# Four of six mask row blocks through a table in DRAM, and the later weights' low parts off TensorE: sparse attention with a two-layer MLP on one core

## The chip, the cores and the metric

The kernel runs on one core of a Trainium2 chip. PE is TensorE (matmuls), DVE is VectorE, ACT is ScalarE, POOL is GpSimd, and SP is SyncE, whose queue issues all the large DMAs here. The metric is the device time of one execution in microseconds, as a median of several runs.

## The reference

Block-sparse attention over 4 batches and 8 heads, 768 tokens, head size 64; its output, as 3072 tokens of 512, goes through a two-layer MLP with a leaky rectifier.

```python
scores = scale * np.matmul(q, k.transpose(0, 1, 3, 2))
mask = np.abs(blk_i - blk_j) <= window          # blocks of 32 tokens, 24 of them
mask = mask | (blk_i == 0) | (blk_j == 0) | (blk_i == n_blocks - 1) | (blk_j == n_blocks - 1)
for qb in range(n_blocks):
    for kb in sampled_blocks[qb]:
        mask[qb * block:(qb + 1) * block, kb * block:(kb + 1) * block] = True
scores = np.where(mask, scores, -1000000000.0)
attn = softmax(scores)
x = (attn @ v), as [3072, 512]
h = x @ w_in                                     # w_in 512 x 2048
g = np.maximum(h, 0.0) + alpha * np.minimum(h, 0.0)
out = g @ w_out                                  # w_out 2048 x 512
```

All inputs and the output are float32.

## The kernel before

**Split numbers.** Every float32 operand of a large product is scaled by a power of two and split into two float16 parts, a high part (the rounded value) and a low part (what is left), and a product is three matmuls: high with high, and each low with the other's high. So each operand needs two instructions: `times` (L431) writes the high part, `rest` (L439) the low part. On DVE the low part is one instruction (L441, reading source and high part), on POOL it is two (L443 scales in place, L444 subtracts).

**The weights.** w_in and w_out come as 16 tiles each, `f` = 0 to 15 (the profile's tensors wi and wo; a tile's raw data stands in a part of wo or in a buffer raw). `raw_to_f32` (L1055) turns a raw tile into float32 in three steps: n1 on DVE (L930), n2 on ACT (L935) or DVE (L940), n3 on DVE (L946). Two or four tiles give a norm over matmuls (gram, L956), and from it the scale. Then `prep_wi` (L1079) and `prep_wo` (L1101) make the two parts. The high part is on ACT, DVE or POOL (L433, L435, L437). The low part of all 16 tiles of w_in, and of the first eight of w_out, comes over PE: POOL scales an identity by the tile's scale (`emit_sid`, L1022), a float32 matmul of it with the tile (L1033) and a float16 matmul of a negative identity with the high part (L1034) leave the difference in PSUM, and ACT copies it out (L1038). The last eight of w_out take `emit_w_lo` on DVE (L441).

**The mask.** A table of 24 x 24 blocks is made on POOL and DVE. PE widens its columns to 768 keys (L380), ACT copies that to `tcol` (L393), 24 rows. For each of the six row blocks t of `bias` (128 queries each, interleaved: query 6p + t), two matmuls with a selection matrix repeat the rows (`mask_rows_pe`, L385) and ACT writes 0 or a large negative number (L401). The code for fewer row blocks on PE stands there already (`MROWS < NT`, L403): a table `rows` of 768 x 768 in DRAM, written from `tcol` with each row 32 times (`mask_store`) and read back by query (`mask_load`). With MROWS = 6 it is not run.

**Attention.** The work is cut in 12 chunks of two query tiles, three to a batch; a chunk has four units (pairs of heads), a unit four steps (one head and one query tile). For each two steps PE makes the scores (L653, L659), DVE adds `bias` and takes the maximum (L669), ACT exponentiates (L676), DVE inverts the sum (L687), p is split into two parts (L433 or L437, then L441 or L443 and L444), SP transposes p by DMA (L704), and at the end of a unit PE multiplies with v (L730); ACT and DVE split that into x (L741, L746).

**The MLP.** For a chunk, eight steps j: PE multiplies x with two tiles of w_in (`emit_up`, L1149, 24 matmuls), DVE applies the rectifier (L1159, L1160), ACT and POOL split the result (L1165, L1170), PE multiplies with two tiles of w_out (`emit_down`, L1191). At the first of them everything of the weights' scales must be there (`emit_gsc`, L993 to L983), since they are one factor of the rectifier.

**What sets the order.** All of this is given to `Plan` as operations with a priority, a choice of engines with costs in us (a pair of numbers marks a step that shares a port between DVE and POOL), dependencies and buffers. `Plan.run` (L119) goes through a time of its own, gives each ready operation to the engine that would end it soonest by these costs (weighted by PREF, and PREF0 up to 130 us), and the kernel's instructions are issued in that order. Each engine then runs its list in order. The constants at L28 to L64 are the priorities and costs.

## Time and profile before

| | |
|---|---|
| median of 3 runs | 816.78 us (816.24 to 818.37) |
| profiled execution, its own time | 818.19 us |
| its span | 816.5 us |
| mean granted clock of PE | 0.985 |
| PE busy | 781.6 us (96%) |
| DVE, ACT, POOL busy | 604.9 (74%), 576.0 (71%), 429.9 us (53%) |
| DMA | 135.35 MB moved, mean 166 GB/s |

Times are from the span's start, in microseconds; instructions that a row groups carry their mean in ns. Short instructions overlap a little on their engine, so a sum of durations is larger than the busy time. A float32 matmul appears as two rows (x2 for one).

### The profile page before, as it was taken

The page shows a single profiled execution, that of the slowest core. Times are in us where ns is not written, and L with a number is a line of the kernel's source. Part 1 is how long each engine was busy: PE and PEld are TensorE (multiplying, and loading weights), DVE is VectorE, ACT ScalarE, POOL GpSimd, SP SyncE. Part 2 cuts the span into 40 slices and gives each one's busy share as a digit, 9 for nine tenths or more (in the row PEclk, how much of TensorE's full clock was granted, in tenths as well). Part 3 has the DMA queues.
Part 4 walks back from the last instruction along what each step waited for, and adds up shares of the span by engine and source line. Part 5 has one row for each costly group of instructions (what it writes and reads, how often), then busy time and mean ns, then how long its engine had stood idle before and what let it go on. Part 6 is the DMA issues. An engine that isn't in the chain of part 4 may idle for free.

```text
span 816.5 us, 16929 instructions
## 1 busy us (share of the span) xinstructions
PE 781.6 (96%) x6335; PEld 504.1 (62%) x6335; DVE 604.9 (74%) x1279; ACT 576.0 (71%) x1041; POOL 429.9 (53%) x360
## 2 busy tenths in 40 slices
PE   6848899999999999999999999999999999999997
PEld 4423365766766666666666666666666666676764
DVE  6898998887689777797687787958687888734231
ACT  6888997897577778876677878736587888724111
POOL 6475786575336555644355655544265656624121
PEclk9978999999999999999999999999999999999999
DMA  9997996987985979879787979629686887643000
GB/s 331 325 310 208 191 184 146 205 161 162 220 193 122 169 162 194 183 153 199 160 174 142 183 179 209 136 77 193 154 204 157 171 171 151 115 97 84 28 1 26
DMA packets 384722, 135.35 MB, mean 166 GB/s; under 512 B 349028, under 2 KB 377728, under 8 KB 384640
## 3 DMA queue, kind: packets, MB, share of 16 engines
q1 hardware_dynamic: 384576, 134.26, 74.8%
q8 instruction: 49, 0.80, 0.4%
q14 instruction: 33, 0.27, 0.1%
q0 software_dynamic: 64, 0.02, 0.0%
HBM read 35.67 MB, written 6.29 MB: 51 GB/s over the span
## 4 chain that ended last, share of the span: by engine, by line
PE 87%; DVE 4%; ACT 3%; POOL 2%; issue 1%; DMA 1%; POOLq 0%; ACTq 0%; DVEq 0%
PE h L1149 30%; PE o L1191 29%; PE sp L730 12%; PE sp L653 7%; PE sp L659 5%; PE d L1033 3%; ACT wo L935 1%; DVE e L669 1%; DMA kf<-in_k_dram 1%; PE d L1034 1%; POOL ph L444 1%; DVE n L930 1%; PE gram L956 0%; DVE ph L441 0%; POOL e L443 0%
## 5 line engine op out<-in xcount | busy, mean ns | idle before, releaser
L1149 PE MATMUL h<-x,wi 128*128 128x256 f16 x2304 | 267.2, 273 | 0.0
L1149 PEld LDWEIGHTS <-wi 128*128 128x128 f16 x2304 | 222.1, 98 | 46.9 <-issue 10.1
L1170 POOL TENSOR_TENSOR gl<-g,gh 128x512 f16<-128x512 f32 x96 | 115.7, 1205 | 220.3 <-ACT gh L1165 192.2
L1191 PE MATMUL o<-wo,gh 128*128 128x512 f16 x768 | 228.9, 380 | 0.0
L669 DVE CUSTOM_DVE_ANT_0 e<-sp,bias,cs 128x768 f32<-128x768 f32 x192 | 191.2, 1010 | 34.7 <-PE sp L659 16.6
L676 ACT ACTIVATE e<-e,nm 128x768 f32<-128x768 f32 x192 | 177.4, 925 | 18.6 <-DVE nm L669 18.4
L444 POOL TENSOR_TENSOR ph<-e,ph 128x768 f16<-128x768 f32 x96 | 171.6, 1788 | 8.0
L433 ACT ACTIVATE ph<-e,rs 128x768 f16<-128x768 f32 x181 | 164.4, 926 | 10.2 <-DVE rs L687 4.9
L443 POOL TENSOR_SCALAR e<-e,rs 128x768 f32<-128x768 f32 x96 | 92.4, 962 | 112.4 <-ACT ph L433 104.9
L1165 ACT CAST gh<-g 128x512 f16<-128x512 f32 x96 | 59.1, 616 | 125.6 <-DVE g L1160 106.0
L1191 PE MATMUL o<-wo,gl 128*128 128x512 f16 x384 | 145.5, 379 | 0.3 <-POOL gl L1170 0.3
L1159 DVE SCALAR_TENSOR_TENSOR g<-h,am 128x512 f32<-128x512 f32 x96 | 66.1, 689 | 78.3 <-PE h L1149 72.2
L1191 PEld LDWEIGHTS <-gh 128*128 128x128 f16 x768 | 70.5, 98 | 82.2 <-issue 6.3
L441 DVE SCALAR_TENSOR_TENSOR ph<-e,rs,ph 128x768 f16<-128x768 f32 x96 | 111.8, 1164 | 8.9 <-ACT ph L433 8.8
L730 PE MATMUL sp<-pt,v 128*64 128x256 f16 x1728 | 103.5, 274 | 0.0
L730 PEld LDWEIGHTS <-v 128*64 128x64 f16 x1728 | 90.6, 110 | 15.7 <-issue 15.0
L1160 DVE SCALAR_TENSOR_TENSOR g<-h,gsc,g 128x512 f32<-128x512 f32 x96 | 72.1, 751 | 3.4
L1191 PEld LDWEIGHTS <-gl 128*128 128x128 f16 x384 | 37.5, 98 | 46.0 <-POOL gl L1170 0.8
L653 PEld LDWEIGHTS <-qt 128*128 128x128 f16 x384 | 37.6, 98 | 29.3 <-issue 7.5
L653 PE MATMUL sp<-kt,qt 128*128 128x512 f16 x192 | 47.5, 330 | 3.6 <-DVE nm L669 3.6
L741 ACT ACTIVATE x<-sp 128x256 f16<-128x256 f32 x48 | 18.3, 380 | 43.6 <-DVE nm L669 25.1
L659 PE MATMUL sp<-kt,qt 64*128 64x512 f16 x192 | 48.2, 332 | 0.0
(152 smaller groups left out, 725.7 us busy)
## 6 DMA issues: line engine op xcount, KB each, us to landing
wo<-in_moe_w_in_dram SPq DMA_DIRECT2D x16, 512.0 KB, 6.4
raw<-in_moe_w_out_dram SPq DMA_DIRECT2D x16, 512.0 KB, 6.6
kf<-in_k_dram SPq DMA_DIRECT2D x16, 384.0 KB, 3.9
qf<-in_q_dram SPq DMA_DIRECT2D x12, 512.0 KB, 4.8
vf<-in_v_dram SPq DMA_DIRECT2D x16, 384.0 KB, 5.3
out_dram<-ob SPq DMA_DIRECT2D x24, 256.0 KB, 2.3
ks<-kt SPq DMA_DIRECT2D x28, 192.0 KB, 3.3
pt<-ph SPq DMA_TRANSPOSE x192, 3.5
```

Of the source, the lines that this page charges most:

```text
L433: nc.scalar.activation(dst, src, AF.Copy, scale=scale)
L441: nc.vector.scalar_tensor_tensor(dst, src, scale, hi, ALU.mult, ALU.subtract)
L443: nc.gpsimd.tensor_scalar(tmp, src, scale, 1.0, ALU.mult, ALU.mult)
L444: nc.gpsimd.tensor_tensor(dst, tmp, hi, ALU.subtract)
L653: nc.tensor.matmul(T["sp", n + i][:, a:z], T["qt", u][:, h, i, :], (ks, kt)[i][:, h, a:z], start=True, stop=False)
L659: nc.tensor.matmul(T["sp", n + i][:, a:z], T["qt", u][r, h, i, :], (kt, ks)[i][r, h, a:z], start=False, stop=True)
L669: nc.vector.tensor_tensor_reduce(T["e", n], T["sp", n], bias[:, t0 + j % w, :], scale=T["cs", c][:, hp : hp + 1], scalar=3.0e38, op0=ALU.a ...
L676: nc.scalar.activation(T["e", n], T["e", n], AF.Exp, bias=T["nm", n], scale=-1.0, accum_out=T["su", n])
L730: nc.tensor.matmul(av[h * D : (h + 1) * D, : n * P], v2[:, h, t, vv, :], T["pt", u, h][:, pl * NT + t, :], start=(m == 0), stop=(m == len( ...
L1149: nc.tensor.matmul(ph[:, i, :], win(w, f, ct), x[:, ct, :], start=(m == 0), stop=(m == len(terms) - 1))
L1170: nc.gpsimd.tensor_tensor(T["gl", c, j], T["g", c, j], T["gh", c, j], ALU.subtract)
L1191: nc.tensor.matmul(T["o", c][t], g[:, i, t * P : (t + 1) * P], wout(w, f), start=(i == 0 and m == 0 and j in first_j), stop=(i == 1 and m ...
```

## The change

The mask: MROWS goes from 6 to 2, so that row blocks 0 and 1 come from PE and ACT as before, and blocks 2 to 5 from the table in DRAM: POOL scales `tcol`, SP writes it with each row 32 times (768 x 768 in bfloat16), and SP reads four row blocks back into `bias`.

The weights: tiles 8 to 15 of w_in take their low parts from `emit_w_lo` on DVE or POOL; the last eight of w_out may now take it on POOL too.

The planner: an operation may have a `lead` (the time after which its DMA is taken to start); the costs are other, and nearly all constants of priority and preference. In the first 22 steps the low part of p may go to DVE or POOL by the planner's choice for each step (`PL0` "d"), where steps had alternated between that choice and DVE alone. A buffer `pa`, not used with HALF = 0, is dropped from the pools.

```diff
-V_WA = -4.856569
-W_WA = 1.529176
+V_WA = 2.696075
+W_WA = 0.554437
...
-PL0 = "dv"
+PL0 = "d"
...
-SLOW = 1.12
+SLOW = 1.02
...
+WI_PE = 8
...
-MROWS = 6
-M_PR = 0.0
+MROWS = 2
+M_PR = 8.0
...
-                        events.append((now + c + 1.0, o.n, "dma", o))
+                        events.append((now + (c + 1.0 if o.lead is None else o.lead), o.n, "dma", o))
...
-    MAX4 = {"DVE": (0.55, 0), "ACT": 0.88, "POOL": 0.95}
-    LOW4 = {"DVE": (0.94, 0), "POOL": (1.1, 1.7)}
+    MAX4 = {"DVE": (0.55, 0), "ACT": 0.88, "POOL": 0.92}
+    LOW4 = {"DVE": (0.96, 0), "POOL": (0.94, 1.52)}
+    LOWW = {"DVE": (0.67, 0), "POOL": (0.75, 1.24)}
...
-            o_sid = plan.op(p + OFF["wh"], {"POOL": 0.5}, lambda g=g: emit_sid(g), [gs[-1]], [sb])
+            if 2 * g < WI_PE:
+                o_sid = plan.op(p + OFF["wh"], {"POOL": 0.41}, lambda g=g: emit_sid(g), [gs[-1]], [sb])
             for y in (2 * g, 2 * g + 1):
...
+                if y >= WI_PE:
+                    prev = o_wi[y] = plan.op(p + OFF["wc"], LOWW, lambda e, y=y: emit_w_lo(e, "wi", y), [o])
+                    continue
                 db = plan.buf("o")
...
-            o_wo[y] = plan.op(p - 3 + 0.1 * (y % HF) + OFF["oh"], {"DVE": (0.67, 0)}, lambda e, y=y: emit_w_lo(e, "wo", y), [o])
+            o_wo[y] = plan.op(p - 3 + 0.1 * (y % HF) + OFF["oh"], LOWW, lambda e, y=y: emit_w_lo(e, "wo", y), [o])
```

Since the planner's costs and constants change, the order moves everywhere; three places matter to the prediction. Line numbers of the changed kernel are up to six higher than those of the kernel before.

PE, at the first up matmul of the MLP, before: the last matmul with v of the fourth unit, a low part of w_in (a scaled identity with a tile, then the negative identity with the high part), and the first up matmul.

```order
L730 MATMUL sp_74<-pt,v_710 64x256
L1033 MATMUL d<-wi,sid 128x512
L1034 LDWEIGHTS wi
L1034 MATMUL d<-wi 128x512
L1149 LDWEIGHTS wi
L1149 MATMUL h<-x,wi 128x256
```

The same place after:

```order
L732 MATMUL sp_74<-pt,v_676 64x256
L1035 MATMUL d<-wo,sid 128x512
L1036 LDWEIGHTS wi
L1036 MATMUL d<-wo,wi 128x512
L1155 LDWEIGHTS wi
L1155 MATMUL h<-x,wi 128x256
```

The first up matmul stands at the same place in both, behind 11 pairs of scores and four units of v; ahead of it stand 14 low parts of w_in before and 8 after, and behind it two before and none after. The low part next to it is now one of w_out.

SP, about the fifth to the tenth load of weights, before (kt, vf, ks, qf are tiles of k, v, swapped k and q; wo takes raw tiles of w_in):

```order
L561 DMA_TRANSPOSE kt<-kn 128x12x128
L469 DMA wo<-in_moe_w_in_dram 128x4x256 x3
L469 DMA vf<-in_v_dram 128x2x384
L561 DMA_TRANSPOSE kt<-kn 128x12x128
L469 DMA vf<-in_v_dram 128x2x384
L469 DMA raw<-in_moe_w_out_dram 128x1024
L469 DMA ks<-kt 64x1536 x2
L469 DMA wo<-in_moe_w_in_dram 128x4x256
L469 DMA raw<-in_moe_w_out_dram 128x1024 x3
L469 DMA qf<-in_q_dram 128x8x128
```

And after:

```order
L563 DMA_TRANSPOSE kt<-kn 128x12x128
L471 DMA wo<-in_moe_w_in_dram 128x4x256
L471 DMA vf<-in_v_dram 128x2x384
L409 DMA rows<-tcol 768x1x768
L471 DMA wo<-in_moe_w_in_dram 128x4x256
L563 DMA_TRANSPOSE kt<-kn 128x12x128
L471 DMA vf<-in_v_dram 128x2x384
L471 DMA wo<-in_moe_w_in_dram 128x4x256
L471 DMA raw<-in_moe_w_out_dram 128x1024
L471 DMA ks<-kt 64x1536 x2
L471 DMA raw<-in_moe_w_out_dram 128x1024 x2
L471 DMA qf<-in_q_dram 128x8x128
```

The write of the table stands behind the first transpose of k; its read (L413) is the next row after these. The loads of weights around them keep nearly their places.

POOL, about where the second unit's p is split, before (e and ph are a step's exponentials and its parts):

```order
L443 TENSOR_SCALAR e<-e,rs 128x768
L444 TENSOR_TENSOR ph<-e,ph 128x768
L1026 TENSOR_SCALAR sid<-wi,swo 128x128
L1022 TENSOR_SCALAR sid<-wi,ssc 128x128
L437 TENSOR_SCALAR ph<-e,rs 128x768
```

After, at the same scaled identity of w_out:

```order
L445 TENSOR_TENSOR ph<-e,ph 128x768
L1028 TENSOR_SCALAR sid<-wi,swo 128x128
L444 TENSOR_SCALAR wi<-wi,ssc 128x512
L445 TENSOR_TENSOR wi<-wi 128x512
L444 TENSOR_SCALAR e<-e,rs 128x768
```

Low parts of w_in, two instructions each, now stand in POOL's order among those of p. Up to its first step of the MLP, POOL has 16 low parts of p (ten before), five of w_in (none before), and four scaled identities of w_in (eight before). DVE has four low parts of p there (ten before), two of w_in (none before) and 13 steps n2 (seven before).

More of the change, by code (lines that the diff above doesn't have):

```diff
@@ L47 @@
 LEADL = 2
[L48 to L50 removed]
+PREF = {"PE": 1.0, "DVE": 4.050975, "ACT": 1.793858, "POOL": 9.673283, "SP": 1.0}
+PREF0 = {"PE": 1.0, "DVE": 1.869151, "ACT": 0.968541, "POOL": 0.404715, "SP": 1.0}
+SLOW = 1.02
 UNTIL = 130.0
 SWITCH = 0.095
[L53 to L55 removed]
+JOIN = 102.510704
+OFF = {"k": -117.65151, "q": -37.496507, "s": -4.929857, "e": 62.087279, "p": -22.695991, "wg": -35.626708, "wh": 119.679285, "wl": 30.953316, "wc": 29.586262, "og": -31.61771, "oh": -0.140414, "ol": 54.958513, "t": 0.0}
+P_AV = 60.371641
 Q_PE = 1
+WI_PE = 8
 N_PS = 6.0
@@ L72, with __init__ @@
 class Op:
-    def __init__(self, n, prio, alts, fn, deps, alloc, use, dma, mode, clear):
-        self.clear = clear
+    def __init__(self, n, prio, alts, fn, deps, alloc, use, dma, mode, clear, lead):
+        self.clear, self.lead = clear, lead
         self.n, self.prio, self.alts, self.fn, self.dma, self.mode = n, prio, alts, fn, dma, mode
@@ L95, in buf, with op @@
         return Buf(pools)
-    def op(self, prio, alts, fn, deps=(), alloc=(), use=(), dma=None, mode=(0, 0), clear=()):
-        o = Op(len(self.ops), prio, alts, fn, deps, list(alloc), list(use), dma, mode, clear)
+    def op(self, prio, alts, fn, deps=(), alloc=(), use=(), dma=None, mode=(0, 0), clear=(), lead=None):
+        o = Op(len(self.ops), prio, alts, fn, deps, list(alloc), list(use), dma, mode, clear, lead)
         for b in o.alloc + o.use:
@@ L1120, in prep_wo @@
         for y in range(x * HF, (x + 1) * HF):
-            o = plan.op(p - 3 + 0.1 * (y % HF) + OFF["oh"], {"ACT": 0.63, "DVE": (0.42, 0), "POOL": 0.75}, lambda e, y=y: emit_w_hi(e, "wo", y), [o_swo[x], o_wo.get(y - 1)])
+            o = plan.op(p - 3 + 0.1 * (y % HF) + OFF["oh"], {"ACT": 0.68, "DVE": (0.42, 0), "POOL": 0.62}, lambda e, y=y: emit_w_hi(e, "wo", y), [o_swo[x], o_wo.get(y - 1)])
             if WO_PE > x:
@@ L1242, in moe @@
         downs, pas = [], []
-        obufs, pbufs = None, [plan.buf("pa") for _ in range(n)] if half else []
+        obufs, pbufs = None, [plan.buf("vf") for _ in range(n)] if half else []
         for i, (kind, j) in enumerate(items):
```

47 lines of the change are left out of this document (21 added, 26 removed).

## The prediction

> **What bounds the kernel now.** I read the page first, for the span in slices.
>
> ```profile
> PE   6848899999999999999999999999999999999997
> DVE  6898998887689777797687787958687888734231
> ```
>
> A slice is 20.4 us. PE has holes in the first five slices and in the last, and none between. So I cut the span where the holes end: at 115.15 us the first up matmul of the MoE (L1149) starts, at 118 us its result is ready for DVE (L1159). The windows view gives busy time per engine for such stretches (length, PE, PEld, DVE, ACT, POOL, then granted clock, DMA share and GB/s):
>
> ```profile
> core 0: us, PE busy (x) PEld busy (x) DVE busy (x) ACT busy (x) POOL busy (x), PEclk, DMA share, GB/s
> 20.00:40.00 20.00, 16.24 (x100) 9.27 (x100) 17.72 (x39) 17.53 (x23) 7.85 (x10) 0.91 1.13 321
> 40.00:60.00 20.00, 9.06 (x60) 4.27 (x58) 19.59 (x41) 17.57 (x26) 16.05 (x13) 0.77 1.14 313
> 0.00:118.00 118.00, 87.83 (x619) 48.93 (x620) 101.91 (x237) 99.74 (x157) 76.19 (x90) 0.90 0.99 262
> 20.00:118.00 98.00, 75.64 (x511) 40.42 (x511) 90.04 (x201) 87.88 (x143) 62.93 (x62) 0.88 1.00 249
> 97.00:115.15 18.15, 17.84 (x154) 10.07 (x154) 17.01 (x49) 17.35 (x33) 14.01 (x14) 1.00 1.08 211
> 115.15:812.00 696.85, 696.52 (x5742) 457.69 (x5740) 505.01 (x1048) 479.08 (x891) 355.45 (x273) 1.00 0.72 150
> ```
>
> After 115.15 PE is busy for 696.52 of 696.85 us: that stage is PE's alone, and a us of PE work taken out of it is a us gained. Before it there are two limits. Up to 118 us DVE is busy 101.91 us and ACT 99.74, PE only 87.83. From 97 to 115.15, though, PE is full (17.84 of 18.15). So the start of the first up matmul, which I call U1, is set by PE at the end of the preparation, and close behind it by DVE. Last I read the chain of waits for the first 118 us, for who stands on it:
>
> ```profile
> by line: PE d L1033 17.7%; PE sp L730 7.1%; ACT wo L935 5.4%; issue 4.9%; PE sp L653 4.1%; DVE n L930 3.6%; PE d L1034 3.5%; PE gram L956 3.3%; ACT e L676 3.0%; PE sp L659 2.9%; ACT ph L433 2.8%; DVE e L669 2.7%; ACT wi L1038 2.5%; PE gkv L
> ```
>
> The weights' low parts on PE (L1033, L1034) are 21.2% of it, some 25 us, and their ACT copies (L1038) 2.5% more. That is where the change cuts.
>
> **The change, part by part.** First PE, from its timeline (start, length):
>
> ```profile
> 22.30 1.46 PE L385 MATMUL sp<-tcol,tok 24*128 24x512 bf16 x4
> 23.69 1.03 PE L956 MATMUL gram<-wi 128*128 128x128 bf16 x8
> 26.64 0.81 PE L385 MATMUL sp<-tcol,tok 24*128 24x512 bf16 x2
> 27.38 0.61 PE L592 MATMUL qp<-wi,qn 128*128 128x128 f16 x4
> 86.61 1.91 PE L1033 MATMUL d<-wi,sid 128*128 128x512 f32 x2
> 113.97 1.12 PE L1033 MATMUL d<-wi,sid 128*128 128x512 f32 x2
> 114.93 0.38 PE L1034 MATMUL d<-wi 128*128 128x512 f16 x1
> 115.15 2.78 PE L1149 MATMUL h<-x,wi 128*128 128x256 f16 x24
> 117.77 1.02 PE L1033 MATMUL d<-wi,sid 128*128 128x512 f32 x2
> 118.85 0.38 PE L653 MATMUL sp<-ks,qt 128*128 128x512 f16 x1
> ```
>
> A mask row block costs PE (23.69 - 22.30) / 2 = 0.70 to 27.38 - 26.64 = 0.74 us. Four go: 2.9 us, all before 28 us, where PE has 3.76 us of idle time in 20 us anyway. I count them at nothing: what follows them waits for DVE and for loads, and if that cover were gone they would be worth 2.9.
>
> A low part costs 115.15 - 113.97 = 1.18 us before U1 and 118.85 - 117.77 = 1.08 after. The eight that go are the last eight of w_in, from the row at 86.61 on: six before U1 (7.1 us) and two behind it (2.2 us). The two lie in the stage that is PE's alone: **2.2 us gained**, with nothing to hide them. The six make room on PE for U1 to come up to 7.1 us sooner, if the other engines let it.
>
> Now those engines, up to the same points in their orders (the first L1159 of DVE, the first L1165 of ACT, the first L1170 of POOL). I counted the rows of both orders and multiplied the differences by these groups (the first six are of the first 118 or 120 us):
>
> ```profile
> L441 DVE SCALAR_TENSOR_TENSOR ph<-e,rs,ph 128x768 f16<-128x768 f32 x10 | 10.7, 1072 | 0.1
> L444 POOL TENSOR_TENSOR ph<-e,ph 128x768 f16<-128x768 f32 x10 | 17.1, 1707 | 0.8
> L443 POOL TENSOR_SCALAR e<-e,rs 128x768 f32<-128x768 f32 x10 | 10.6, 1061 | 3.8 <-ACT ph L433 3.5
> L437 POOL TENSOR_SCALAR ph<-e,rs 128x768 f16<-128x768 f32 x10 | 10.3, 1027 | 9.2 <-DVE rs L687 5.5 <-ACT dn L681 3.6
> L437 POOL TENSOR_SCALAR wi<-wi,ssc 128x512 f16<-128x512 f32 x12 | 8.3, 694 | 9.5 <-PE d L1033 9.5
> L940 DVE SCALAR_TENSOR_TENSOR n<-raw,n 128x512 int32<-128x512 int32 x3 | 2.1, 687 | 0.0
> L441 DVE SCALAR_TENSOR_TENSOR wo<-wo,swo 128x512 f16<-128x512 f32 x8 | 6.1, 761 | 0.5 <-ACT wo L433 0.5
> L1170 POOL TENSOR_TENSOR gl<-g,gh 128x512 f16<-128x512 f32 x96 | 115.7, 1205 | 220.3 <-ACT gh L1165 192.2
> L1022 POOL TENSOR_SCALAR sid<-wi,ssc 128x128 f32<-128x128 f32 x8 | 3.6, 456 | 7.8 <-PE d L1033 6.7 <-DVE ssc L424 1.0
> L1038 ACT CAST wi<-d 128x512 f16<-128x512 f32 x16 | 9.9, 620 | 4.0 <-PE d L1034 3.7 <-PE gram L966 0.4
> L935 ACT ACTIVATE raw<-raw 128x512 uint16<-128x512 uint16 x13 | 17.5, 1366 | 2.4 <-DVE n L930 2.3
> L401 ACT ACTIVATE bias<-sp 128x768 bf16<-128x768 f32 x6 | 4.8, 832 | 0.0
> 6.19 0.62 DVE L435 TENSOR_SCALAR kn<-kf,ks 128x768 f16<-128x768 f32 x1
> 49.91 2.06 DVE L435 TENSOR_SCALAR v<-vf,sv 128x768 f16<-128x768 f32 x1
> ```
>
> ACT: seven casts go (7 x 0.62 = 4.3), six of the L935 go to DVE (8.2), four mask copies go (3.3): 15.8 us less; six more high parts of w_in and four fewer of p, near the same size, leave it there. ACT stops being a limit.
>
> DVE: six more n2 (L940, 4.1), two low parts of w_in (1.5), about three more high parts (at most 0.62 each, 1.9) and five tiny ones (0.8), against six fewer low parts of p (6.4), one fewer high part of v (2.06) and two copies that ACT takes (some 1 us): -1.2 us, or nothing if the small ones are larger. I take **0.5 us gained**. So DVE has as much to do before U1 as it had.
>
> POOL: six more pairs L443 and L444 for p (16.6), five pairs for w_in (no row; the nearest, L437 and L1170 of that width, give 1.9 each, 9.5), three more high parts of p (3.1), a part of q and the scaling of the mask table (some 5), less six high parts of w_in (4.2) and four scaled identities (1.8): 28 us more, 76.19 + 28 = 104 by the time that DVE takes up U1's result. POOL had 42 us of room and has about 14.
>
> What is late next is therefore DVE. Between 20 and 118 us it idles 98.00 - 90.04 = 7.96 us. With ACT lighter, PE lighter by 7.1 and the low parts no longer passing from PE to ACT and back, some of that goes; all of it at best, nothing at worst. I take half: **U1 4.0 us sooner**.
>
> DVE next to POOL has a price of its own. The 128x768 scaling took 0.62 us alone and 2.06 us where POOL's pair on v ran beside it, 1.44 us lost. The Trainium skill ("SBUF — State Buffer", section "Who interferes with whom") says that VectorE and GpSimd share a port pair as an exclusive lock, and that a VectorE instruction in a two-port mode or with two SBUF inputs waits out a GpSimd instruction that started first; the two rows agree. By that rule, each of the 12 added POOL pairs could cost DVE as much, 17.3 us in all; by the row of L441 beside POOL's work (1.072 mean) DVE's usual price is below 0.1 us. I take nothing in the sum, since DVE itself has fewer such instructions than before (four low parts of p instead of ten), and keep the rest as a rival.
>
> The table costs DMA: 768 x 768 x 2 bytes written, 1.18 MB, and 128 x 3072 x 2 read, 0.79 MB, at the 313 to 321 GB/s of the rows above: 3.7 + 2.5 = 6.2 us, and they fall where the DMA engines are fully taken (1.13 and 1.14). The mask rows themselves are first needed by the ninth pair of scores (the first row below), and hide. The loads queued behind them on SP do not quite: the other rows are a load of w_in, its landing time as a median, and the DVE step that reads it.
>
> ```profile
> 100.54 0.49 PE L653 MATMUL sp<-ks,qt 128*128 128x512 f16 x2
> 48.09 0.54 SPq L469 DMA_DIRECT2D wo<-in_moe_w_in_dram  x1
> wo<-in_moe_w_in_dram SPq DMA_DIRECT2D x16, 512.0 KB, 6.4
> 59.13 0.67 DVE L930 TENSOR_SCALAR n<-wo 128x512 int32<-128x512 int32 x1
> ```
>
> 59.13 - 48.09 - 6.4 = 4.6 us of slack against 6.2: 0 to 1.6 us late. I take **0.5 us lost**. The Trainium skill ("DMA: Bandwidth & Descriptors", section "Why a DMA increments its semaphore by 16 and not by 1") lets a DMA use the largest number of engines up to 16 that divides both outer sizes; with a source of 24 rows that is 12, and the store would take 3.7 x 16 / 12 = 5.0 us and the loss reach 2.9. No row of this trace shows it.
>
> SP's wait for the scaled table also adds little: the transpose of k that stands ahead of the store there waits for POOL's step just before the table's.
>
> Sum: 4.0 + 2.2 + 0.5 - 0.5 = 6.2 us sooner. The profiled execution took 818.19 us (span 816.5), 1.4 above the median of 816.78; 818.19 - 6.2 = 812.0 for it, and by the median **810.6**. A measurement of this kernel can tell about 0.3%, 2.45 us, from no change.
>
> **The rivals.**
>
> (a) PE's whole saving comes off: 2.9 + 7.1 + 2.2 = 12.2 us, 804.6. For it: on the chain up to 118 us the low parts on PE have 21.2%, DVE's two largest entries (L930, L669) 6.3% together. Against it: U1 would have to come 10 us sooner, and DVE has only 7.96 us of idle time after 20 us and must do as much. Chance 0.20.
>
> (b) DVE sets U1 where it is: only the two low parts behind U1 count, 816.78 - 2.2 = 814.6. For it: equal DVE work, and idle times that have many causes. Against it: ACT and PE, which it waits for, get 15.8 and 7.1 us lighter. Chance 0.18.
>
> (c) POOL takes from DVE what PE gave: each of the 12 added pairs holds up DVE, or DVE's data, between 20 and 115 us. At 1.44 us each it is 17.3, so 810.6 + 17.3 = 827.9; the point at which it decides is 6.2 / 12 = 0.5 us for each, and 0.75 makes the kernel slower by 9.0 - 6.2 = 2.8. For it: the row of 2.06, and POOL with 104 of 118 us taken, so that a late p has no slack. Against it: six of the ten DVE instructions that read two SBUF operands there are gone, and L940 kept 0.687 us. Chance 0.16.
>
> That the change doesn't do what it says can be left out: the new order has eight low parts of w_in on PE instead of 16, three of the other eight on DVE and five on POOL, and two mask row blocks.
>
> **How the numbers follow.** My forecast, U1 about 4 us sooner and 810.6, has 0.46; its own ends are U1 1 to 7 us sooner, so 813.6 to 807.6. With (a) at 0.20, (b) at 0.18 and (c) at 0.16, faster takes 0.46 + 0.20 and a third of (b), 0.06: 0.72. Same takes the rest of (b), 0.12, and 0.03 of (c): 0.15. Slower keeps 0.13. The range reaches down past (a) by a us, since a granted clock or a shorter DVE list could add to it: 803.6. Upward it holds (b), and the loss of 2.9 us on the loads with it, 817.5. Left out are (c), and what lies below (a).
>
> **What would show it.** In the profile of the changed kernel: the first up matmul at 108 to 114 us; PE busy without a hole behind it; from there to the end 2.2 us less than now; DVE's idle time between 20 us and U1 at about 4 us; POOL over 100 us busy by then; DVE's scalings near 0.62 and no L930 waiting for a load. It is wrong if U1 starts at 115 us or later, if PE idles behind U1 for want of POOL's low parts, or if U1 starts before 107, which would mean that DVE had more room than its busy time says.

## The result, and the profile after

The changed kernel takes 823.79 us (median of 4 runs, 823.32 to 824.13) where the kernel before took 816.54 beside it (816.24 to 818.37): a ratio of 1.0080, 95% interval 1.0067 to 1.0092. It is 7.2 us slower between the medians, 6.5 by the ratio. The forecast was 810.6 and its range ended at 817.5: wrong in sign and in size.

The profiled execution took 823.88 us, with a span of 821.8. That of the kernel before, with 818.19, was one of its longer ones, so the two profiles lie only 5.7 us apart. Here are PE and DVE of the changed kernel in the 40 slices of the page.

```profile
PE   5757679999999999999999999999999999999997
DVE  6987999888768888788888777787887766664231
```

PE now has holes in the first six slices instead of five, and deeper ones. These are stretches of the changed kernel, with the columns as before (length, PE, PEld, DVE, ACT, POOL, granted clock, DMA share, GB/s):

```profile
20.00:40.00 20.00, 14.18 (x81) 7.37 (x80) 18.82 (x40) 11.69 (x17) 11.03 (x13) 0.67 1.10 235
40.00:60.00 20.00, 12.14 (x71) 5.67 (x68) 17.16 (x41) 16.40 (x26) 18.06 (x14) 0.76 1.10 305
0.00:122.96 122.96, 82.03 (x576) 46.49 (x577) 103.31 (x238) 85.76 (x133) 99.22 (x107) 0.81 1.05 267
97.00:115.15 18.15, 14.05 (x110) 7.46 (x109) 16.85 (x40) 14.99 (x30) 17.65 (x16) 0.91 1.13 248
122.96:821.80 698.84, 693.93 (x5728) 456.99 (x5727) 521.63 (x1068) 468.43 (x869) 348.98 (x271) 1.00 0.73 150
```

ACT did get lighter (11.69 us between 20 and 40, where it had 17.53; up to U1 by 11.1 us of the 15.8 that were forecast), but DVE did not (18.82, where it had 17.72), and PE's granted clock there fell from 0.91 to 0.67. From 97 to 115.15 us PE was full before; now it idles 4.1 of 18.15 us, and POOL is the full one (17.65). The place where the time goes is U1, on PE's timeline of the changed kernel:

```profile
115.79 2.15 PE L732 MATMUL sp<-pt,v 128*64 128x256 f16 x35 [0.38 <-DMA pt<-ph]
117.87 1.12 PE L1035 MATMUL d<-wo,sid 128*128 128x512 f32 x2
119.05 0.49 PE L1155 MATMUL h<-x,wi 128*128 128x256 f16 x3
120.78 0.60 PE L1155 MATMUL h<-x,wi 128*128 128x256 f16 x4 [1.24 <-ACT x L743]
122.96 4.64 PE L1155 MATMUL h<-x,wi 128*128 128x256 f16 x41 [1.58 <-DVE uq L422]
```

U1 is issued at 119.05, stops twice for the parts of x, and runs on only from 122.96, where it started at 115.15 before: 7.8 us later. Behind that point the span has 821.8 - 122.96 = 698.8 us left, where it had 816.5 - 115.15 = 701.4: 2.5 us less. So the span is 7.8 - 2.5 = 5.3 us longer. Seven of U1's 24 matmuls are already done at 122.96, at 2.78 / 24 = 0.116 us each. Counted for the same matmul, U1 is 7.0 us later and the rest 1.7 us shorter.

The loss can be placed more closely. The second unit's product with v starts at 91.80 us before and at 91.65 after: up to there the two kernels are level. The whole loss arises between it and U1, and it grows on the way: the tenth pair of scores starts 1.2 us later than before (107.87 against 106.67), the eleventh 2.1 (112.84 against 110.71), and the fourth unit's product with v ends 3.9 later (117.94 against 114.05). The other 3.1 us of the 7.0 are U1 waiting for x. That stretch in the kernel before:

```profile
91.80:115.15 23.35, 22.07 (x204) 13.13 (x202) 22.11 (x59) 22.34 (x43) 16.14 (x17) 1.00 1.11 210
```

and in the changed kernel:

```profile
91.65:122.96 31.31, 22.77 (x205) 13.64 (x204) 29.80 (x65) 24.17 (x45) 30.64 (x28) 0.95 0.97 214
```

Before, PE, DVE and ACT were all busy for about 22 of 23.35 us. After, DVE does 29.80 us of work and POOL 30.64 in 31.31. DVE's 7.7 us more are about the 8.0 us by which the stretch has grown. I call this stretch, from the second unit's product with v to U1, the last stretch below. What DVE does in the few us ahead of U1, on the timeline of the changed kernel:

```profile
115.45 0.95 DVE L999 TENSOR_SCALAR ro<-ro,s_wo 128x2 f32<-128x2 f32 x1
116.53 0.75 DVE L1002 TENSOR_SCALAR rg<-rg,s_wi 128x8 f32<-128x8 f32 x1
117.31 0.83 DVE L1004 TENSOR_TENSOR gsc<-rg,ro 128x8 f32<-128x8 f32 x1
118.18 0.85 DVE L985 TENSOR_TENSOR am<-al,gsc 128x16 f32<-128x16 f32 x1
118.96 0.74 DVE L442 SCALAR_TENSOR_TENSOR wi<-wi,ssc 128x512 f16<-128x512 f32 x1
119.62 2.39 DVE L442 SCALAR_TENSOR_TENSOR ph<-e,rs,ph 128x768 f16<-128x768 f32 x1
122.50 0.40 DVE L748 SCALAR_TENSOR_TENSOR x<-sp,x 128x256 f16<-128x256 f32 x1
```

The last row writes the part of x that U1 was waiting for (PE's row names the short step right behind it, which ends at 122.96). U1 needs neither of the two low parts that stand ahead of it in DVE's list, at 118.96 and 119.62: DVE's low parts of w_in are of tiles 8 to 15, which a later up step reads, and the four units' products with v are done by 117.94. From 118.96 to 122.01 they take 3.1 us, as much as U1 waits. ACT's part of x is late by the first of them as well: a high part of w_in that must follow it stands ahead of x in ACT's list and waits 1.97 us for it, until 119.73. The same steps in the kernel before, grouped over its last stretch (mean in ns):

```profile
L441 DVE SCALAR_TENSOR_TENSOR ph<-e,rs,ph 128x768 f16<-128x768 f32 x3 | 3.0, 1008 | 0.0
L1000 DVE TENSOR_SCALAR rg<-rg,s_wi 128x8 f32<-128x8 f32 x1 | 0.5, 541 | 0.0
L997 DVE TENSOR_SCALAR ro<-ro,s_wo 128x2 f32<-128x2 f32 x1 | 0.3, 289 | 0.0
L983 DVE TENSOR_TENSOR am<-al,gsc 128x16 f32<-128x16 f32 x1 | 0.2, 174 | 0.0
L1002 DVE TENSOR_TENSOR gsc<-rg,ro 128x8 f32<-128x8 f32 x1 | 0.2, 167 | 0.0
```

The four tiny steps took 1.17 us in sum and take 3.38; the low part of p took 1.01 and takes 2.39. POOL has no gap in that time:

```profile
114.73 1.64 POOL L445 TENSOR_TENSOR ph<-e,ph 128x768 f16<-128x768 f32 x1
116.34 1.79 POOL L438 TENSOR_SCALAR ph<-e,rs 128x768 f16<-128x768 f32 x2
118.11 0.91 POOL L444 TENSOR_SCALAR e<-e,rs 128x768 f32<-128x768 f32 x1
119.10 2.10 POOL L445 TENSOR_TENSOR ph<-e,ph 128x768 f16<-128x768 f32 x1
```

These end at 116.37, 117.25 and 118.13 (the two of the second row), 119.02 and 121.20. Each tiny step ends 0.01 to 0.03 us behind one of the first four (116.40, 117.28, 118.14, 119.03), and the low part of p ends 0.81 us behind the last. In the kernel before, POOL had a gap of 0.40 us at 111.87, and the last two tiny steps started in it and took 0.17 each. So 3.6 us are the same instructions, longer because they wait for POOL's. The Trainium skill ("SBUF — State Buffer", "Who interferes with whom") says that VectorE and GpSimd share a port pair that one locks against the other; these rows agree. Most of the rest of DVE's 7.7 us is work that is new there or has come later:

```profile
L442 DVE SCALAR_TENSOR_TENSOR ph<-e,rs,ph 128x768 f16<-128x768 f32 x3 | 5.0, 1682 | 0.3 <-POOL ph L438 0.3
L442 DVE SCALAR_TENSOR_TENSOR wi<-wi,ssc 128x512 f16<-128x512 f32 x2 | 1.9, 954 | 0.0
L948 DVE SCALAR_TENSOR_TENSOR wi<-wo,n 128x512 int32<-128x512 int32 x2 | 1.4, 675 | 0.0
```

Two low parts of w_in (1.9), more conversions of weights than before (the row of 1.4 had no counterpart in the last stretch before), and three low parts of p at 5.0 us instead of 3.0, of which 1.4 us are counted already. Together: 2.2 + 2.0 + 1.9 + 1.4 = 7.5 of the 7.7 us.

### The profile page after: what moved, and what is told of

Same layout as the page of the kernel before. It is cut to its first block, busy times and chain, and to the rows that moved or that the text cites. A ratio compares the mean times of both kernels' runs of the same rounds, so it can differ in the third digit from the quotient of the medians.

```text
span 821.8 us, 16856 instructions
## 1 busy us (share of the span) xinstructions
PE 776.0 (94%) x6303; PEld 503.5 (61%) x6303; DVE 624.9 (76%) x1305; ACT 554.2 (67%) x1002; POOL 448.2 (55%) x377
## 4 chain that ended last, share of the span: by engine, by line
PE 50%; DMA 1%; ACT 0%; DVE 0%; issue 0%; DVEq 0%; ACTq 0%
PE o L1197 19%; PE h L1155 19%; PE sp L732 6%; PE sp L655 4%; PE sp L661 2%; DMA pt<-ph 1%; DMA kf<-in_k_dram 0%; ACT e L678 0%; DVE e L671 0%; ACT junk L430 0%; DVE ob L1212 0%; PE tot L521 0%; ACT x L743 0%; PE bc L617 0%; DVEq L1212 0%
## 5 line engine op out<-in xcount | busy, mean ns | idle before, releaser
L444 POOL TENSOR_SCALAR e<-e,rs 128x768 f32<-128x768 f32 x101 | 97.4, 965 | 189.9 <-ACT ph L434 170.3
L445 POOL TENSOR_TENSOR ph<-e,ph 128x768 f16<-128x768 f32 x101 | 175.9, 1741 | 8.4
L434 ACT ACTIVATE ph<-e,rs 128x768 f16<-128x768 f32 x167 | 151.1, 926 | 11.6 <-DVE rs L689 5.4
L442 DVE SCALAR_TENSOR_TENSOR ph<-e,rs,ph 128x768 f16<-128x768 f32 x91 | 115.8, 1274 | 7.0 <-ACT ph L434 6.5
L732 PE MATMUL sp<-pt,v 128*64 128x256 f16 x1728 | 106.1, 277 | 4.7 <-DVE nm L671 4.3
L732 PEld LDWEIGHTS <-v 128*64 128x64 f16 x1728 | 92.7, 111 | 20.9 <-issue 20.1
L655 PE MATMUL sp<-ks,qt 128*128 128x512 f16 x192 | 48.3, 334 | 1.9 <-DVE nm L671 1.9
```

The costliest lines, as they stand in the source:

```text
L434: nc.scalar.activation(dst, src, AF.Copy, scale=scale)
L442: nc.vector.scalar_tensor_tensor(dst, src, scale, hi, ALU.mult, ALU.subtract)
L444: nc.gpsimd.tensor_scalar(tmp, src, scale, 1.0, ALU.mult, ALU.mult)
L445: nc.gpsimd.tensor_tensor(dst, tmp, hi, ALU.subtract)
L655: nc.tensor.matmul(T["sp", n + i][:, a:z], T["qt", u][:, h, i, :], (ks, kt)[i][:, h, a:z], start=True, stop=False)
L732: nc.tensor.matmul(av[h * D : (h + 1) * D, : n * P], v2[:, h, t, vv, :], T["pt", u, h][:, pl * NT + t, :], start=(m == 0), stop=(m == len( ...
```

## The experiments

Four theories stood against each other. **D**: the table's DMA holds up SP's queue and the loads. **P**: POOL, with 12 more pairs, is full and late. **V**: DVE's list in the last stretch sets U1. **R**: the new order of instructions is worse as a whole. Ratios are to runs of the kernel before on the same chip, with their 95% interval. Kernels with the order kept differ from their parent only in the rows named. With the plan kept, the named steps also change their engine or their place. b_table and b_lowparts were planned anew.

| kernel | parent | median us | before beside it | ratio |
|---|---|---|---|---|
| no_table | changed, order kept | 823.87 | 817.23 | 1.0083 (1.0063 to 1.0103) |
| store_only | changed, order kept | 822.64 | 817.23 | 1.0081 (1.0052 to 1.0110) |
| b_table | before, new order | 823.97 | 817.23 | 1.0087 (1.0065 to 1.0108) |
| b_lowparts | before, new order | 833.90 | 817.23 | 1.0209 (1.0190 to 1.0228) |
| hi_on_act | changed, plan kept | 823.47 | 817.47 | 1.0074 (1.0059 to 1.0090) |
| n2_on_act | changed, plan kept | 824.31 | 817.47 | 1.0085 (1.0069 to 1.0101) |
| no_pool_low | changed, plan kept | 823.32 | 817.47 | 1.0068 (1.0050 to 1.0086) |
| b_pool_load | before, order kept | 829.27 | 817.47 | 1.0145 (1.0126 to 1.0164) |
| defer | changed, plan kept | 833.67 | 817.09 | 1.0200 (1.0184 to 1.0216) |
| defer_hi | changed, plan kept | 832.83 | 817.09 | 1.0190 (1.0165 to 1.0215) |
| defer_hi_n2 | changed, plan kept | 836.12 | 817.09 | 1.0233 (1.0215 to 1.0252) |
| b_dve_load | before, order kept | 823.10 | 817.09 | 1.0074 (1.0057 to 1.0090) |
| less_dve | changed, order kept | 821.10 | 817.49 | 1.0043 (1.0025 to 1.0061) |
| spread | changed, plan kept | 830.63 | 817.49 | 1.0163 (1.0145 to 1.0182) |
| b_two_low | before, order kept | 817.25 | 817.49 | 0.9994 (0.9985 to 1.0003) |
| b_eight_low | before, order kept | 822.22 | 817.49 | 1.0050 (1.0035 to 1.0065) |
| b_none_low | before, order kept | 818.91 | 817.28 | 1.0021 (1.0012 to 1.0030) |
| b_table_kept | before, order kept | 820.24 | 817.28 | 1.0034 (1.0021 to 1.0048) |

**The table taken out of the changed kernel.**

```diff
+    nc.vector.memset(bias[:, MROWS:, :], 0.0)
...
-        o = plan.op(M_PR, {"SP": 0.47}, mask_store, [o], [], [pbuf2], dma=3.6)
-        o = plan.op(M_PR, {"SP": 0.47}, mask_load, [o], [], [], dma=2.4)
+        o = plan.op(M_PR, {"SP": 0.47}, lambda e: None, [o], [], [pbuf2], dma=3.6)
+        o = plan.op(M_PR, {"SP": 0.47}, lambda e: None, [o], [], [], dma=2.4)
```

no_table: 

> The changed kernel with its order of instructions kept on every engine, but the write of the table and its read back are not issued; mask blocks 2 to 5 are filled once with zeros by DVE at the start, so this kernel leaves out the mask in four of six row blocks. Theory D (the table's 1.95 MB of DMA, issued at 25 to 32 us, hold up SP's queue and the loads behind it): the second transpose of k takes about 5 us instead of 10.2, U1 runs without a break from about 115 us instead of 122.96, and the time is 814 to 817 us. Theory P (POOL, with 12 more pairs of low parts, is full and late): nothing of this changes, 822 to 824 us. Theory R (the new order itself is the worse one): 822 to 824 us as well.

store_only keeps the first of the two lines: 

> As no_table, but the write of the table is issued and only its read back is not; mask blocks 2 to 5 are zeros, so the mask is left out there. Theory D in its first form (the write from 24 rows is the slow one and stands ahead of the transpose of k): 821 to 824 us, with the transpose still at about 10 us. Theory D in its second form (all bytes count alike): the write is 60 per cent of the bytes, so about 60 per cent of the loss against no_table. P and R: the same time as no_table, 822 to 824 us.

The write does hold up SP's queue. SP's rows of the changed kernel:

```profile
25.13 0.97 SPq L409 DMA_DIRECT2D rows<-tcol  x1
26.78 10.21 SPq L563 DMA_TRANSPOSE kt<-kn  x1
```

and of no_table, where the same transpose follows no write of the table:

```profile
25.91 4.16 SPq L564 DMA_TRANSPOSE kt<-kn  x1
```

The transpose gets 6 us faster, and the kernel not at all: 1.0083 against 1.0080 with the table, U1 runs on from 122.11 instead of 122.96. DVE's fill takes 1.34 us at the start, where DVE waits for the first loads anyway. Theory D falls for the changed kernel: the delay is there, and something else is later. store_only is the same within its interval, so it can't tell the two forms of D apart.

**Each part alone, planned anew.** b_table sets MROWS = 2 and M_PR = 8.0 in the kernel before; b_lowparts gives it the changed lines of prep_wi with WI_PE = 8.

b_table: 

> The kernel before with the table alone: two mask row blocks from PE and four through DRAM, all low parts of w_in on PE as before; the planner makes the order anew with the old costs. Theory D: slower than the kernel before by most of what the whole change lost behind its gain, 820 to 826 us. P and R: 815 to 818 us, as the kernel before.

b_lowparts: 

> The kernel before with the second part alone: low parts of w_in tiles 8 to 15 on DVE or POOL, the mask as before; the planner makes the order anew with the old constants. Theory D: it keeps the 2.2 us behind U1 and something ahead of it, 811 to 815 us. Theory P: POOL and DVE are late with p, U1 comes later than 115 us, 818 to 824 us. Theory R leaves it open, since this order is a third one.

Both are slower than before, b_lowparts by more than the whole change. Each has an order of its own, with constants fitted to neither, so they tell only that a new order can cost as much as what is looked for. The later experiments therefore keep the order.

**POOL relieved, DVE relieved, POOL loaded.**

```diff
 hi_on_act
-        hi = plan.op(..., lambda e: emit_p_hi(e, n), [o], [pb], [eb])
+        hi = plan.op(..., lambda e: emit_p_hi("ACT" if e == "POOL" and n < NS0 else e, n), [o], [pb], [eb])
 n2_on_act
-            o = plan.op(..., lambda e: emit_n2(e, name, f, 0), [o], [], bufs + [tb])
+            o = plan.op(..., lambda e: emit_n2("ACT" if f % 2 else e, name, f, 0), [o], [], bufs + [tb])
 no_pool_low
-    lambda e, y=y: emit_w_lo(e, "wi", y)
+    lambda e, y=y: emit_w_lo(e, "wi", y) if e == "DVE" else nc.vector.memset(wparts("wi", y)[2], 0.0)
 b_pool_load (kernel before)
             emit_p_lo(e, n)
+            if e == "POOL" and n < NS0:
+                nc.gpsimd.tensor_scalar(T["e", n], T["e", n], 1.0, 1.0, ALU.mult, ALU.mult)
+                nc.gpsimd.tensor_tensor(T["ph", n][:, 1, :], T["e", n], T["ph", n][:, 0, :], ALU.subtract)
```

hi_on_act: 

> The changed kernel; the plan is kept, but the eleven high parts of p that the plan gives to POOL in the first 22 steps are issued on ACT (at the same place of the plan), so POOL has 11 x 0.91 = 10 us less and ACT as much more. Theory P (POOL's list has no gap from 36 to 77 and from 82 to 123 us in the changed kernel, and sets U1): U1 comes 5 to 10 us sooner, 814 to 819 us. Theory V (DVE, 97 per cent busy from 80 to 120 us, sets U1): 822 to 824. Theory R (the order of PE is the worse one, whatever the engines do): 822 to 824.

n2_on_act: 

> The changed kernel; the plan is kept, but the seven n2 steps of odd weight tiles that the plan gives to DVE are issued on ACT, as the kernel before had most of them: DVE has 7 x 0.69 = 4.8 us less, ACT 9.6 us more, POOL the same. Theory V: U1 comes 3 to 5 us sooner, 819 to 821 us. Theories P and R: 822 to 824 us.

no_pool_low: 

> The changed kernel; the plan is kept, but the five low parts of w_in that POOL makes are left out and filled with zeros by DVE, so this kernel leaves out five of sixteen low parts. POOL has 5 pairs of 1.9 to 2.4 us less, 8 to 10 us, all behind 85 us. Theory P: U1 4 to 8 us sooner, 816 to 820. Theories V and R: 822 to 824.

b_pool_load: 

> The kernel before with its order kept; behind each of the eleven low parts of p that POOL makes in the first 22 steps, POOL does the pair once more (the same result written again): 11 x 2.56 = 28 us more work on POOL up to U1, as much as the change adds, and nothing else. Theory P: slower by 4 to 12 us, 820 to 829. Theories V and R: POOL has 42 us of room, so 816 to 819.

None of the three reliefs brings U1 sooner: it runs on from 123.99, 124.09 and 123.67 us. So POOL alone is not the bound of the changed kernel, and P falls as a single cause, with a reserve: the reliefs brought costs of their own. In hi_on_act ACT becomes the full one (29.15 of 31.80 us below). In each of the three one product with v ran slowly in the last stretch (3.82, 3.71 and 3.87 us, where the changed kernel has 2.15), and PE's mean granted clock there is 0.87 to 0.89 instead of 0.95. 1.6 to 1.7 us of a relief may be hidden by that. n2_on_act took one of its seven steps out of the last stretch (one n2 is left there, of two) and the others out of the part ahead of it, which was level anyway; in the stretch DVE waited 2.2 us for ACT's slower steps. V's 819 to 821 us are missed, but it says little about V. The last stretches of the three:

```profile
92.19:123.99 31.80, 24.12 (x204) 14.78 (x203) 28.13 (x65) 29.15 (x51) 22.54 (x20) 0.89 0.97 207
```
```profile
92.44:124.09 31.65, 24.28 (x205) 14.73 (x203) 28.88 (x64) 25.34 (x46) 28.00 (x26) 0.89 0.87 199
```
```profile
91.43:123.67 32.24, 24.73 (x204) 15.00 (x203) 28.57 (x66) 23.69 (x44) 23.16 (x21) 0.87 0.90 203
```

DVE is still busy for 28 to 29 of 32 us in each: POOL's load fell by up to 8 us there and DVE's by one or two. On the kernel before, b_pool_load's eleven pairs cost 11.8 us, although POOL had 42 us without work; nine of them, 24.5 us, run ahead of U1. V and R had expected nothing, P 820 to 829 us. Its last stretch:

```profile
93.65:122.49 28.84, 23.89 (x204) 13.75 (x202) 24.38 (x59) 22.82 (x42) 27.66 (x27) 0.94 0.76 176
```

Here POOL is the full one, 27.66 of 28.84 us. Of its 42 idle us only 23.35 - 16.14 = 7.2 lay in the last stretch, so the rest was no room for what has to be done there.

**DVE's list in the last stretch.** In b_dve_load three low parts of p are done three times; in less_dve DVE's five low parts there are replaced by fills.

```diff
 b_dve_load (kernel before)
-        lo = plan.op(..., lambda e: emit_p_lo(e, n), ...)
+            for _ in range(3 if e == "DVE" and 13 <= n <= 17 else 1):
+                emit_p_lo(e, n)
 less_dve (changed kernel)
     def emit_p_lo(e, n):
+        if e == "DVE" and 10 <= n <= 20:
+            nc.vector.memset(T["ph", n][:, 1, :], 0.0)
+            return
...
-    lambda e, y=y: emit_w_lo(e, "wi", y)
+    lambda e, y=y: emit_w_lo(e, "wi", y) if e == "POOL" else nc.vector.memset(wparts("wi", y)[2], 0.0)
```

b_dve_load: 

> The kernel before with its order kept; three low parts of p on DVE, all between the second unit's product with v and the weights' scales, are done three times each (the same result): 6 x 1.0 = 6 us more on DVE in that stretch, nothing else. Theory V (DVE is busy 22.1 of 23.4 us there): slower by 5 to 6 us, 822 to 823. Theory R: the wait falls into gaps of the other engines, 817 to 819.

less_dve: 

> The changed kernel; the plan is kept, but the five low parts that DVE makes between the second unit's product with v and the weights' scales (three of p, two of w_in; 5.0 and 1.9 us there) and the few behind them are left out and filled with zeros, so part of the low parts is missing. DVE does 6.9 - 1.7 = 5.2 us less in that stretch, nothing else changes. Theory V (DVE's list in that stretch): U1 4 to 5 us sooner, 818 to 820 us. Theory R (waits between engines in an unlucky order): 822 to 824.

b_dve_load is 6.0 us slower for six more low parts; the nine take 10.7 us in the stretch, where three took 3.0. Its last stretch, to the start of U1:

```profile
91.47:120.60 29.13, 23.87 (x203) 13.85 (x202) 27.64 (x60) 22.21 (x42) 18.14 (x17) 0.94 0.74 162
```

DVE has 5.5 us more than in the kernel before and the stretch is 5.8 us longer. Behind 120.60 U1 does seven matmuls and waits once more for DVE's x, until 122.48. less_dve:

```profile
91.79:119.83 28.04, 22.77 (x206) 13.89 (x205) 24.48 (x67) 24.33 (x45) 26.36 (x26) 0.94 1.08 239
```

With 5.3 us less on DVE the stretch is 3.3 us shorter. U1 starts at 118.61 and has x at 119.6 instead of 122.96, since DVE writes it at 119.16, behind fills where the two low parts stood. The kernel is at 1.0043 instead of 1.0080: 3 us back. That misses V's 818 to 820 by a us, and R's 822 to 824 by as much. V holds for the kernel before; in the changed kernel DVE's list accounts for 3.3 of the 7.0 us, nearly all of it in the steps that stand ahead of x. DVE now idles 28.04 - 24.48 = 3.6 us of the stretch, where it had idled 1.2 in the kernel before, so something else is next, and the rest of the loss isn't shown to be DVE's load.

**Putting w_in's later low parts off.** U1 reads only the first two tiles of w_in; the parts of tiles 8 to 15 are first read by the fifth up step.

```diff
     for o in plan.run():
+        if o in late and ups < 3:
+            held.append(o)
+            continue
+        emit(o)
+        if o in o_up0:
+            ups += 1
+            for x in held[:5] if ups < 3 else held:
+                emit(x)
+            held = held[5:] if ups < 3 else []
...
```

defer: 

> The changed kernel; the plan is kept, but the eight low parts of w_in tiles 8 to 15 and the seven high parts that must follow them are issued only behind the first, second and third up matmul step (five at a time), on the engines that the plan gave them to. The fifth up step is the first that reads them. Up to the second unit's product with v (91.7 us) the changed kernel is level with the kernel before; behind it, up to U1, DVE is busy 29.8 of 31.3 us (before 22.1 of 23.4). Theory V (DVE's list in that stretch sets U1; each us taken out of it comes off, and POOL's pairs lengthen DVE's own instructions): DVE loses two low parts and a high part there (2.6 us) and the stretch beside four POOL pairs, so U1 3 to 5 us sooner, 818 to 821. Theory R (the order of PE and the waits between engines set it, no single list): 822 to 824. Theory P: as no_pool_low, 822 to 824.

defer_hi: 

> defer, and the high parts of p that POOL makes in the first 22 steps issued on ACT as well (POOL 10 us less again). If POOL and DVE hold each other up, so that relieving one shows nothing while the other stays: U1 5 to 8 us sooner than in the changed kernel, 815 to 819. Theory R: 822 to 824.

defer_hi_n2: 

> defer_hi, and the seven n2 steps of odd tiles on ACT instead of DVE (DVE 4.8 us less, ACT 9.6 more). Theory V: 1 to 3 us sooner than defer_hi, as long as ACT, with about 105 of 120 us taken, is not late. Theory R: as defer_hi, or later, since the steps on ACT are twice as long.

spread: 

> As defer, but the fifteen parts put off are issued one at a time, six planned steps apart, behind the first up matmul, and a tile's two parts are both on POOL (even tiles) or both on DVE (odd ones), so that DVE does not stand waiting for ACT in front of the rectifier. In defer U1 ran on from 119.73 us instead of 122.96, and then PE idled 7 us between 120 and 140. If the loss of defer was only that lump: U1 at 119 to 120 and no hole behind it, 819 to 821 us. If putting them off is itself too dear for DVE and POOL behind U1: 824 to 832.

In defer U1 starts at 118.64 and runs through without a wait, so its eighth matmul, for which the changed kernel waits until 122.96, comes some 3.5 us sooner, as V expected for this stretch. (The 119.73 in spread's expectation is the first row of a view that begins at 120, not a start of U1.) But the kernel is 10 us slower than the changed one. Its PE behind U1:

```profile
126.81 0.49 PE L655 MATMUL sp<-ks,qt 128*128 128x512 f16 x2 [2.76 <-DVE nm L671]
136.16 0.60 PE L1201 MATMUL o<-wo,gh 128*128 128x512 f16 x2 [2.08 <-ACT gh L1175]
138.13 0.61 PE L1201 MATMUL o<-wo,gl 128*128 128x512 f16 x1 [1.37 <-POOL gl L1180]
```

The parts that were put off form a chain (each high part waits for the low part ahead of it), and in DVE's row they stand in front of the rectifier: DVE once waited 5.84 us for ACT there. spread takes the lump apart and still loses: PE waits 5.07 us for POOL's low part of the rectifier's result at 146.65. defer_hi and defer_hi_n2 change nothing of that. defer and defer_hi miss every time that was expected; defer_hi_n2 is later than defer_hi, which R allowed, and spread falls into the second of its cases, putting off being itself too dear. Two different things stand behind that. In spread DVE is full from 120 to 140 us (19.64 of 20). In defer it is busy for only 9.60 of these 20 us and POOL for 13.40, so the chain of waits costs there, not a lack of room. No version tried was faster than the kernel before.

**The forecast's gain by itself, on the kernel before.** All three keep its order; only the eight low parts of tiles 8 to 15 (b_two_low: the two behind U1) leave PE and ACT. In the cut, `moved` stands for the tiles of each kernel, with the engine that takes them.

```diff
 emit_w_lo_pe(name, f, db)
+        if name == "wi" and f in moved:
+            return
 emit_w_lo_copy(name, f)
-        nc.scalar.copy(lo, T["d", name, f])
+        if name == "wi" and f in moved:
+            rest(moved[f], lo, w, s, hi, w)          # b_two_low, b_eight_low
+            nc.gpsimd.memset(lo, 0.0)                # b_none_low, in place of it
+        else:
+            nc.scalar.copy(lo, T["d", name, f])
```

b_two_low: 

> The kernel before with its order kept; only the two low parts of w_in that stand behind U1 on PE (117.77 and 122.65 us, with their ACT copies) are made by POOL instead, at the place of the copy. The term of the forecast that all theories share: PE is full there and nothing else is, so 2.2 us come off: 814 to 815.5 us.

b_eight_low: 

> The kernel before with its order kept; the eight low parts of w_in tiles 8 to 15 are made by POOL (six) and DVE (two) at the place of the ACT copy, and PE leaves them out. This is the second part of the change without a new order. The forecast's way (PE's room lets U1 come sooner): 808 to 812. Theory V (DVE full in the last stretch; two low parts more and POOL's six pairs lengthen its own instructions): U1 not sooner, 815 to 820.

b_none_low: 

> The kernel before with its order kept; the eight low parts of w_in tiles 8 to 15 are not made at all: PE leaves out their matmuls, ACT their copies, and POOL fills them with zeros at the place of the copy, so this kernel leaves out half the low parts of w_in. PE has 9.3 us less (7.1 ahead of U1, 2.2 behind), ACT 5 us less, DVE the same. This is the forecast's gain without its cost. The forecast: U1 4 us or more sooner and 2.2 us behind it, 809 to 811 us. Theory V (DVE sets the pace until well behind U1, PE's low parts lie in its shadow): 0 to 2.5 us off, 815 to 817.5.

b_two_low gains nothing that can be measured, against 2.2 us that all theories expected. PE, which had no gap there before, now has these:

```profile
121.13 0.48 PE L653 MATMUL sp<-ks,qt 128*128 128x512 f16 x2 [0.21 <-DVE nm L669]
122.07 0.48 PE L653 MATMUL sp<-kt,qt 128*128 128x512 f16 x2 [0.45 <-DVE nm L669]
129.13 0.48 PE L653 MATMUL sp<-kt,qt 128*128 128x512 f16 x2 [1.04 <-DVE x L746]
```

1.7 of the 2.2 us turn into waits for DVE. b_none_low goes furthest: PE has 781.6 - 772.7 = 8.9 us less to do, ACT 3 us less, DVE the same, and the kernel is 1.6 us slower than before (818.91 against 817.28). Its preparation and the 25 us behind it:

```profile
0.00:115.00 115.00, 78.56 (x583) 44.58 (x584) 99.49 (x229) 94.57 (x146) 76.47 (x93) 0.81 0.98 265
115.00:140.00 25.00, 23.09 (x186) 15.11 (x186) 23.20 (x51) 20.12 (x40) 20.01 (x19) 1.00 0.86 144
```

PE is busy for 78.56 of 115 us where it was 84.83, and DVE for 99.49 where it was 98.95. U1 is issued at 113.06, waits, and the score pair that stood at 135.99 stands at 135.15: 0.8 us sooner. That is all that arrives of 9 us, and in b_two_low, where PE keeps its work ahead of U1, the same pair stands at 135.20. The last stretch of b_none_low, from the second unit's product with v to where U1 runs on:

```profile
89.79:115.91 26.12, 19.10 (x196) 12.53 (x195) 24.03 (x62) 20.94 (x39) 20.25 (x24) 0.93 0.95 204
```

It begins 2.0 us sooner than before and is 2.8 us longer, with DVE 1.9 us busier in it, and PE idles 7.0 us of it. The run is not free of costs of its own: POOL's eight fills are 4.2 us of new work, and the four tiny DVE steps, which wait for POOL, take 2.83 us in sum here instead of 1.17. Even if all 4.2 us had delayed U1, 4.2 - 1.6 = 2.6 of the 9 us would have come off (an estimate). b_eight_low adds the real work, two low parts on DVE and six pairs on POOL: 4.1 us slower (0.0050 of 817.5), above the 815 to 820 of V and far from the forecast's 808 to 812. Its last stretch:

```profile
90.15:118.28 28.13, 19.16 (x195) 12.31 (x194) 27.75 (x63) 21.25 (x40) 23.97 (x26) 0.94 0.93 193
```

DVE is busy for 27.75 of 28.13 us, PE for 19.16: DVE sets its length, and its low parts of p have a mean of 1.60 us.

**The table alone, with the order kept.**

```diff
 b_table_kept (kernel before)
     def mask_rows_pe(t):
+        if t > 1:
+            return
...
+        if t == 1:
+            nc.gpsimd.tensor_scalar(tcol, tcol, -NEG, NEG, ALU.mult, ALU.add)
+            nc.sync.dma_start(rows.rearrange("(b r) s -> b r s", r=BLK), ...)
```

The read back stands ahead of the first transpose of p. 

> The kernel before with its order kept; mask row blocks 2 to 5 come from the table (POOL scales it and SP writes it behind the second row block, SP reads it back ahead of the first transpose of p), and PE and ACT leave their rows out. This is the first part of the change without a new order. Theory V and no_table (the table is hidden either way): 816 to 818.5 us. If the table's DMA does hold up the kernel before: 820 to 824, as b_table.

It is 1.0034 (1.0021 to 1.0048), 2.8 us slower, at the lower edge of what D expects; V missed. The loads behind the write do come late, on DVE's timeline:

```profile
36.72 0.69 DVE L944 TENSOR_SCALAR n<-wo 128x512 int32<-128x512 int32 x1 [3.33 <-DMA wo<-in_moe_w_in_dram]
```

Before, no n1 step waited for a load between 20 and 60 us. Of the 3.3 us, 1.3 are left at U1 (116.42 against 115.15); the last stretch is unchanged (23.34 us, DVE 22.19). The profiled execution was the fastest of six (818.85), so its 1.3 may be a low figure. So the table costs something in the order before; in the new one, which is late for other reasons, no cost of it could be measured.

## Why the prediction was wrong, step by step

**U1 4.0 us sooner: the step that failed.** U1 came 3.9 us later, and ran on 7.0 us later. The prediction put half of DVE's idle time of 7.96 us between 20 and 118 us as the gain, because PE and ACT, for which DVE waits, got lighter. b_none_low makes them lighter, with POOL's fills as its only new work; 0.8 us arrives behind U1, nothing at the end, and by the estimate above 2.6 us at most without the fills. In the changed kernel DVE's idle time between 20 us and U1 is 102.96 - 91.11 = 11.9 us, not the 4 that the prediction named as a sign. The idle time that counted was that of the last stretch, 23.35 - 22.11 = 1.2 us. PE was full there too, but with work that filled its waits for DVE: without that work it idles 7.0 us there. The chain of waits went through these low parts because they ended last, not because anything was held up by them. Rows that were on the page, PE, ACT and DVE full over the same 18 us (17.84, 17.35 and 17.01), were read as PE first and DVE "close behind it"; they were a tie, and a tie gives next to nothing for one side's work.

**2.2 us behind U1: nearly the right size, at the wrong place.** For the same matmuls the changed kernel needs 1.7 us less behind U1. Yet b_two_low shows that this term isn't worth 2.2 us by itself: the stage was PE's alone on the average over 697 us, and in its first 15 us DVE is right behind PE. In the changed kernel U1 is late enough for DVE to have caught up; that is the likely reason, not one that a run shows.

**DVE 0.5 us less, and nothing for POOL beside it: wrong.** Up to U1 DVE was busy 99.10 us before and 103.31 after. The counts were right (four low parts of p, two of w_in, 13 n2); the durations were those of before. Low parts of p went from 1.07 to 1.59 us in the mean, 2.1 us for the four, and the four tiny steps to the scales from 1.17 to 3.38 us in sum: 4.3 of the 4.7 us by which the term was off. The sum put the price of POOL beside DVE at nothing because fewer low parts of p stood on DVE; the tiny steps, which pay it too, were not counted.

**POOL at 104 us, 14 us of room: the size right, the conclusion wrong.** It had done 102.2 us when DVE took up U1's result (at 126.05). But its room was counted over 118 us. In the last stretch POOL had 7.2 us idle before and has 31.31 - 30.64 = 0.7. b_pool_load, which put its pairs into the 42 idle us, paid 11.8 us for them.

**Loads 0.5 us late, 0 to 1.6:** with the order kept one is 3.3 us late for DVE, outside the bounds; 1.3 us of it are left at U1, and the kernel is 2.8 slower. In the changed kernel they cost nothing that no_table could show.

**Rival (c), POOL takes from DVE, was the one that came closest,** with a chance of 0.16: right in its mechanism, too large in its price (827.9), and without DVE's tiny steps. DVE's steps ahead of U1 show 3.6 us of it. The rest is DVE's new and later work, the order in which x stands behind it, and PE's gain that did not exist. Rival (b) gave 814.6 for U1 unchanged; b_two_low, which is just that case with two pairs on POOL, gave 817.25.

**What is left open.** With the order kept, the two parts cost 2.8 and 4.1 us, 6.9 in sum, and the whole change 6.5 (0.0080 of 816.5). That looks like a sum and is not one: in the changed kernel the table costs nothing that could be measured. less_dve gives back 3 us; how much of the rest its new order makes, as against the moved work, was not separated, and no kernel with the changed constants and all low parts on PE was run. Theory R is not refuted for that share.

## What to carry to other kernels

Where two engines are both full over the stretch that sets a milestone, taking work from one gives little more than the other's idle time in that stretch, however much the chain of waits passes through the first: take the milestone's last 20 us, not the average of the stage, and compare busy with length for every engine. Work that fills an engine's waits is free there, and moving it to an engine that is waited for costs about its length (six low parts on DVE cost 6.0 us here). Where two engines hold each other up, count every instruction that pays, the tiny ones too. Look also at what stands in an engine's list just ahead of the step that others wait for. Before believing a gain, leave the work out altogether: if nothing comes off (1.0021 here for 9 us of PE), moving it elsewhere has little to gain.
